# Reordering a cold-start stage and moving a logarithm off ScalarE: one change in two places of a spectral-mixing and memory-attention kernel

## The chip, the cores and the metric

One core of a Trainium2 chip. The metric is device time in microseconds (us), median of several executions. The classes are faster, same and slower at 2%.

## The reference, cut to what matters

Two pairs of layers over 2048 tokens of width 640, each layer reading a layer norm of the running x:

```python
x = A_x                                            # 2048 x 640, bf16
x = x + A(layernorm(x), A_w_r, A_w_i)              # rfft2, times a complex weight, irfft2
x = x + B(layernorm(x), mem0, Wq, Wk, Wv, Wo)      # 64 segments of 32 tokens + 8 memory tokens, 32 heads
x = x + A(layernorm(x), ...)
x = x + B(layernorm(x), ...)
# layernorm: (x - mean) / sqrt(var + 1e-5), without scale and bias
```

Most of the time is layer B's matmuls. The change concerns two things only: the start of the first layer A (the **cold stage**, from the start of the program until the first matmul of the spectrum, `ab`), and the layer norm between A and B (the two **token stages**, one for each pair of layers).

## The kernel before

The cold stage doesn't normalize x. It scales the DFT table of each 128-token tile by 1/sigma and takes the mean off with two small matmuls per tile. The 16 tiles fall into five rows, `groups`; a row's 1/sigma needs the statistics of all its tiles. Statistics come from VectorE (DVE) with `bn_stats` twice and `bn_aggr` once, or from two passes on ScalarE (ACT) for tiles 3, 7 and 11. The order of issue is written by hand:

```python
    def cold_raw(self, x_src, s3):
        ...
        groups = [(0, 4), (4, 8), (8, 12), (12, 14), (14, 16)]
        by_act = (3, 7, 11)
        ...
        def scales(q):
            a, b = groups[q]
            sl, v = slice(a, b), mv[:, a:b, 1]
            small = nc.gpsimd if q < 4 else nc.vector
            nc.scalar.activation(out=r0[:, sl], in_=v, func=ACTF.Ln, bias=g["eps"][:, 0:1])
            nc.scalar.activation(out=r0[:, sl], in_=r0[:, sl], func=ACTF.Exp, scale=-0.5)
            ...                       # one Newton step and the hi/lo parts of the mean, on `small`

        def stats(t):
            for hlf in range(2):
                nc.vector.bn_stats(out=st[:, t % 2, hlf, :], in_=x[:, t, hlf * 320:(hlf + 1) * 320])
            nc.vector.bn_aggr(out=mv[:, t, :], in_=st[:, t % 2, :, :])

        def scale_tables(q):
            for t in range(*groups[q]):
                nc.vector.tensor_scalar_mul(out=Ts[:, t, :], in0=T[:, t, :], scalar1=rs[:, t:t + 1])
        ...                           # matmuls(q): 60 (or 30) small matmuls; empties(q, ...): evictions of results from PSUM (PE's result memory), A = ACT, D = DVE
        with tc.manual_schedule(engines={...}):
            act_stats(3)
            for t in (0, 1, 2):
                stats(t)
            scales(0)
            ...
            act_stats(7)
            for t in (4, 5):
                stats(t)
            scale_tables(0)
            ps0 = matmuls(0)
            stats(6)
            scales(1)
            act_stats(11)
            for t in (8, 9):
                stats(t)
            scale_tables(1)
            empties(0, ps0, "AA")
            ps1 = matmuls(1)
            ...
            for t in (12, 13):
                stats(t)
            scales(3)
            ...
            empties(3, ps3, "AADAD")
            ps4 = matmuls(4)
            empties(4, ps4, "DADAD")
```

In a token stage tokens come in pairs. ACT evicts each token twice (`Gs` at L586, `x` at L603); DVE takes its statistics; `_ln_inverse` makes 1/sigma of the pair; DVE normalizes (`norm`, L130).

```python
def _ln_inverse(nc, pool, mv, nt, eps_t, small):
    ...
    nc.scalar.activation(out=r0, in_=mv[:, :nt, 1], func=ACTF.Ln, bias=eps_t[:, 0:1])     # L112
    nc.scalar.activation(out=r0, in_=r0, func=ACTF.Exp, scale=-0.5)                        # L113
    if small is nc.vector:
        ...                                                    # three instructions
    else:
        small.tensor_scalar_add(out=t, in0=mv[:, :nt, 1], scalar1=LN_EPS)                  # L120, then Newton
        small.tensor_tensor(out=t, in0=t, in1=r0, op=ALU.mult)
    small.tensor_tensor(out=t, in0=t, in1=r0, op=ALU.mult)
    small.tensor_scalar(out=t, in0=t, scalar1=-0.5, scalar2=1.5, op0=ALU.mult, op1=ALU.add)
    small.tensor_tensor(out=t, in0=t, in1=r0, op=ALU.mult)
...
            for i in range(16 + 1):                            # the token stage's order
                last = i >= 13
                if i >= 2 and last:
                    stats(i - 2)
                if i >= 5 and i % 2 == 1:
                    norm((i - 5) // 2)
                if i >= 2 and not last:
                    stats(i - 2)
                if i < 16:
                    spectrum_d(i)
                if 1 <= i <= 16:
                    tokens(i - 1)
                if i >= 4 and i % 2 == 0:
                    inverse((i - 4) // 2, nc.gpsimd)
```

## Time and profile before

| | before |
|---|---|
| median of 4 runs (lowest to highest) | 1559.09 us (1558.63 to 1559.90); the first three, which the prediction had, 1558.79 |
| span of the profiled execution | 1557.3 us |
| start to first `ab` matmul (S) | 26.56 us |
| first token stage (first psg to first psq matmul) | 42.54 us |
| second token stage | 42.55 us |

The last three rows are starts of matmuls, taken from the timeline of TensorE (PE). They are the lengths that the change can touch. The prediction below shows the page, the cold timeline and the chain of waits. Here is DVE's timeline in the cold stage (columns: start, length, engine, line, operation, output and input with their shapes, and in brackets the idle time before with its releaser):

```profile
7.79 0.89 DVE L313 BATCH_NORM_STATS2 A1xn_S<-A1x_S 128x6 f32<-128x320 bf16 x2 [0.74 <-DMA A1x_S<-in_A_x_dram]
8.71 0.21 DVE L314 BATCH_NORM_AGGREGATE A1xn_S<-A1xn_S 128x2 f32<-128x12 f32 x1
8.84 0.83 DVE L313 BATCH_NORM_STATS2 A1xn_S<-A1x_S 128x6 f32<-128x320 bf16 x2
```

Tile 4 reaches DVE 0.74 us late, from DRAM, while the tables of row 0 stand behind it in the queue.

### The profile page before, as it was taken

The page shows a single profiled execution, that of the slowest core. Times are in us where ns is not written, and L with a number is a line of the kernel's source. Part 1 is how long each engine was busy: PE and PEld are TensorE (multiplying, and loading weights), DVE is VectorE, ACT ScalarE, POOL GpSimd, SP SyncE. Part 2 cuts the span into 40 slices and gives each one's busy share as a digit, 9 for nine tenths or more (in the row PEclk, how much of TensorE's full clock was granted, in tenths as well). Part 3 has the DMA queues.
Part 4 walks back from the last instruction along what each step waited for, and adds up shares of the span by engine and source line. Part 5 has one row for each costly group of instructions (what it writes and reads, how often), then busy time and mean ns, then how long its engine had stood idle before and what let it go on. Part 6 is the DMA issues. An engine that isn't in the chain of part 4 may idle for free.

```text
span 1557.3 us, 36583 instructions
## 1 busy us (share of the span) xinstructions
PE 1531.2 (98%) x14482; PEld 1077.5 (69%) x14483; DVE 815.5 (52%) x2414; ACT 771.7 (50%) x2251; POOL 234.4 (15%) x327
## 2 busy tenths in 40 slices
PE   7999999999999999999999999999999999999998
PEld 5776666666666666777777776666666666667775
DVE  7873545665556555633367545655556545553111
ACT  5584555556555565511127655556555565562000
POOL 3520111112111121100034101112111121110000
PEclk9999999999999999999999999999999999999999
DMA  4681344444433433645114523443533434327241
GB/s 171 222 304 30 111 151 140 137 140 134 160 131 137 148 125 145 203 116 169 51 50 165 174 69 125 137 150 124 179 123 137 146 125 171 124 101 233 75 132 51
DMA packets 168694, 214.88 MB, mean 138 GB/s; under 512 B 8128, under 2 KB 134088, under 8 KB 168512
## 3 DMA queue, kind: packets, MB, share of 16 engines
q1 hardware_dynamic: 167936, 210.15, 41.0%
q8 instruction: 115, 1.88, 0.5%
q0 software_dynamic: 576, 2.30, 0.4%
q14 instruction: 67, 0.55, 0.1%
HBM read 167.32 MB, written 45.10 MB: 136 GB/s over the span
## 4 chain that ended last, share of the span: by engine, by line
PE 94%; DVE 2%; ACT 1%; DMA 1%; issue 1%; POOL 1%; SPq 0%; DVEq 0%; POOLq 0%; ACTq 0%
PE psv L1201 19%; PE psk L1135 18%; PE psx L1481 18%; PE psq L1135 18%; PE pso L1285 4%; PE pss L1211 4%; PE ab L427 2%; PE psg L585 1%; PE psl L1238 1%; PE psq L1159 1%; PE X L458 1%; PE psu L519 1%; PE psm L911 1%; DMA bB_S<-in_B_Wk_dram 1%; PE psg L1642 1%
## 5 line engine op out<-in xcount | busy, mean ns | idle before, releaser
L1135 PEld LDWEIGHTS <-bB_S 128*128 128x128 bf16 x3180 | 261.7, 97 | 181.6 <-DMA bB_S<-in_B_Wk_dram 1.1
L1194 DVE CAST bB_S<-psk 128x495 bf16<-128x495 f32 (+3 forms) x320 | 191.8, 599 | 281.2 <-PE psk L1135 276.7
L1481 PE MATMUL psx<-Wo_sb,bB_S 128*128 128x320 bf16 x2048 | 288.7, 299 | 0.1
L1214 ACT ACTIVATE bB_S<-pss 128x269 bf16<-128x269 f32 (+5 forms) x576 | 208.4, 386 | 138.2 <-PE pss L1211 137.9
L1481 PEld LDWEIGHTS <-bB_S 128*128 128x128 bf16 x2048 | 196.8, 98 | 73.9 <-DVE bB_S L1299 0.7
L1179 ACT ACTIVATE bB_S<-psq 128x96 bf16<-128x96 f32 x300 | 152.4, 508 | 172.2 <-PE psq L1135 172.2
L1254 POOL TENSOR_TENSOR bB_S<-bB_S,bB_S 128x535 f32<-128x535 f32 x90 | 111.7, 1255 | 795.2 <-DVE bB_S L1246 762.2
L1299 DVE TENSOR_TENSOR bB_S<-pso,bB_S 128x480 bf16<-128x480 f32 (+1 forms) x320 | 193.1, 603 | 55.6 <-PE pso L1285 44.9
L1215 DVE TENSOR_TENSOR bB_S<-bB_S,maskf 128x269 bf16<-128x269 bf16 (+5 forms) x576 | 159.4, 290 | 114.4 <-ACT bB_S L1214 114.4
L1203 ACT CAST bB_S<-psv 128x512 bf16<-128x512 f32 (+1 forms) x288 | 162.6, 564 | 80.9 <-PE psv L1201 80.9
L1201 PE MATMUL psv<-bB_S,B1hT_S 128*128 128x256 bf16 x1360 | 168.8, 272 | 0.0
L1201 PE MATMUL psv<-bB_S,B2hT_S 128*128 128x256 bf16 x1360 | 168.8, 272 | 0.0
L1135 PE MATMUL psk<-B2hT_S,bB_S 128*128 128x495 bf16 (+3 forms) x800 | 164.2, 343 | 0.0
L1135 PE MATMUL psk<-B1hT_S,bB_S 128*128 128x495 bf16 (+3 forms) x800 | 164.2, 343 | 0.0
L1135 PE MATMUL psq<-B1hT_S,bB_S 128*128 128x495 bf16 (+5 forms) x780 | 156.1, 336 | 0.6 <-DMA bB_S<-in_B_Wk_dram 0.5
L1135 PE MATMUL psq<-B2hT_S,bB_S 128*128 128x495 bf16 (+5 forms) x780 | 156.1, 336 | 0.5 <-DMA bB_S<-in_B_Wk_dram 0.5
L1201 PEld LDWEIGHTS <-B2hT_S 128*128 128x128 bf16 x1360 | 129.8, 98 | 24.3
L1201 PEld LDWEIGHTS <-B1hT_S 128*128 128x128 bf16 x1360 | 129.8, 98 | 24.3
L1211 PE MATMUL pss<-bB_S 128*128 128x132 bf16 (+8 forms) x1152 | 137.5, 219 | 0.0
L1211 PEld LDWEIGHTS <-bB_S 128*128 128x128 bf16 x1152 | 95.4, 97 | 55.1
L1285 PE MATMUL pso<-bB_S,bB_S 128*128 128x132 bf16 (+8 forms) x1152 | 118.6, 219 | 0.2
L1285 PEld LDWEIGHTS <-bB_S 128*128 128x128 bf16 x1152 | 89.7, 98 | 32.2 <-DVE oTmf L1300 1.8
(293 smaller groups left out, 1422.0 us busy)
## 6 DMA issues: line engine op xcount, KB each, us to landing
bB_S<-Rd SPq DMA_DIRECT2D x124, 535.0 KB
oTx_d<-bB_S SPq DMA_DIRECT2D x60, 512.0 KB
bB_S<-oTx_d SPq DMA_DIRECT2D x46, 512.0 KB
bB_S<-in_B_Wq_dram SPq DMA_DIRECT2D x32, 320.0 KB
bB_S<-in_B_Wk_dram SPq DMA_DIRECT2D x32, 320.0 KB
bB_S<-in_B_Wv_dram SPq DMA_DIRECT2D x32, 320.0 KB
Wo_sb<-in_B_Wo_dram SPq DMA_DIRECT2D x4, 1280.0 KB
B1wv_S<-in_B_Wv_dram SPq DMA_DIRECT2D x10, 512.0 KB
```

The lines of the kernel that those rows point to most:

```text
L1135: nc.tensor.matmul(ps, lhsT=w[:, ch, hh * 128:(hh + 1) * 128], rhs=src[:, ch, lo:hi], start=(ch == 0), stop=(ch == 4))
L1179: nc.scalar.mul(out=qv[:, :, 0:SEG], in_=x_view(ps, o, n)[:, :, 1:SW], mul=scale)
L1194: nc.vector.tensor_copy(out=KTs[h % 2][:, lo:hi], in_=ps[:, 0:hi - lo])
L1201: nc.tensor.matmul(ps[:, i * 256:(i + 1) * 256], lhsT=hT[:, ch, st.hcol((t + i) * 128):st.hcol((t + i) * 128) + 128], rhs=w["Wv"][:, ch, : ...
L1203: nc.scalar.copy(out=V[:, t:t + n, :].rearrange("p a b -> p (a b)"), in_=ps[:, 0:n * 256])
L1211: nc.tensor.matmul(ps[:, off - o0:off - o0 + hi - lo], lhsT=KT[:, t * 128:(t + 1) * 128], rhs=QT[:, lo:hi], start=True, stop=True)
L1214: nc.scalar.activation(out=E[:, 0:n], in_=ps[:, 0:n], func=ACTF.Exp)
L1215: nc.vector.tensor_tensor(out=P[:, o0:o0 + n], in0=E[:, 0:n], in1=bs.mask[:, o0:o0 + n], op=ALU.mult)
L1254: nc.gpsimd.tensor_tensor(out=acc, in0=acc, in1=part, op=ALU.add)
L1285: nc.tensor.matmul(pso[:, lo - q0:hi - q0], lhsT=V[:, t, (h % 2) * 128:(h % 2 + 1) * 128], rhs=P[:, off:off + hi - lo], start=(i == 0), st ...
L1299: nc.vector.tensor_tensor(out=oT.rearrange("p (r s j) -> p r s j", r=16, j=2)[:, :, s0:s0 + ns, :], in0=byclass(po), in1=rx, op=ALU.mult)
L1481: self.tc.nc.tensor.matmul(ps[:, 0:320], lhsT=lhs(h, k // 2), rhs=self.g["Wo_sb"][:, h, c0:c0 + 320], start=(h == 0), stop=(h == H - 1))
```

## The change

Its intent: in the cold stage, let PE start earlier and at full clock, and keep DVE and ACT from waiting for one another; in the token stages, take the logarithm and the exponential out of ACT's queue by computing (var + eps)^-0.5 with `pow` on GpSimd. The core of the diff:

```diff
+def _inverse(nc, g, t, r0, v, small):
     if small is nc.vector:
+        nc.scalar.activation(out=r0, in_=v, func=ACTF.Ln, bias=g["eps"][:, 0:1])
+        nc.scalar.activation(out=r0, in_=r0, func=ACTF.Exp, scale=-0.5)
         ...
+        return
+    small.tensor_scalar_add(out=t, in0=v, scalar1=LN_EPS)
+    small.tensor_tensor(out=r0, in0=t, in1=g["half"][:, 0:t.shape[1]], op=ALU.pow)    # half holds -0.5
+    small.tensor_tensor(out=t, in0=t, in1=r0, op=ALU.mult)                            # Newton step as before
     ...
-            if a in (4, 8):                       # loads of the tables
-                nc.sync.dma_start(out=T[:, 2 * a - 8:2 * a, :], ...)
+            if a in (2, 4, 8):
+                c, d = (a // 4 * 4, b) if a < 8 else (8, 16)
+                nc.sync.dma_start(out=T[:, c:d, :], ...)
-        by_act = (3, 7, 11)
+        by_act = (3, 7, 11, 13)
+        idle = pp.tile([128, 4, 128], FP32, name="idle", tag="pa")
+        for i in range(WARM):                     # WARM = 96
+            nc.tensor.matmul(idle[:, i % 4, :], lhsT=g["ones"][:], rhs=g["ones"][:], start=True, stop=True)
+        def logs(q):                              # Ln and Exp of a row, now on their own
+            flush()
+            ...
         def scales(q):
-            small = nc.gpsimd if q < 4 else nc.vector
-            ...                                   # Ln, Exp; Newton on small
+            ...                                   # Newton on DVE, means on GpSimd
         def stats(t):
-            for hlf in range(2):
-                nc.vector.bn_stats(out=st[:, t % 2, hlf, :], ...)
-            nc.vector.bn_aggr(out=mv[:, t, :], in_=st[:, t % 2, :, :])
+            nc.vector.bn_stats(out=st[:, t % 2, 0, :], ...)
+            flush()                               # the bn_aggr of the tile before
+            nc.vector.bn_stats(out=st[:, t % 2, 1, :], ...)
+            pending.append(t)
         def scale_tables(q):                      # tables 2 and 3 of row 0 go to ACT
-            act_stats(7)
-            for t in (4, 5):
-                stats(t)
             scale_tables(0)
             ps0 = matmuls(0)
-            stats(6)
+            act_stats(7)
+            for t in (4, 5, 6):
+                stats(t)
+            logs(1)
+            stats(8)
             scales(1)
+            scale_tables(1)
+            ps1 = matmuls(1)
+            empties(0, ps0, "AA")
+            act_stats(11)
             ...                                   # likewise for rows 2 to 4: logs(q), one more tile, scales(q)
+            act_stats(13)
+            logs(3)
```

More of the change, by code (lines that the diff above doesn't have):

```diff
@@ L20 @@
 S, D = 2048, 640
+WARM = 96
 NF = 321
@@ L105, in _ln_stats, with _ln_inverse @@
     nc.vector.bn_aggr(out=mv[:, t, :], in_=st[:, t % 2, :, :])
-def _ln_inverse(nc, pool, mv, nt, eps_t, small):
+def _ln_inverse(nc, pool, mv, nt, g, small):
     rs = pool.tile([128, 4], FP32, name="lnrs", tag="lnrs", bufs=3)
     nb = pool.tile([128, 4], FP32, name="lnnb", tag="lnnb", bufs=3)
-    t, r0 = rs[:, :nt], nb[:, :nt]
-    nc.scalar.activation(out=r0, in_=mv[:, :nt, 1], func=ACTF.Ln, bias=eps_t[:, 0:1])
-    nc.scalar.activation(out=r0, in_=r0, func=ACTF.Exp, scale=-0.5)
+    _inverse(nc, g, rs[:, :nt], nb[:, :nt], mv[:, :nt, 1], small)
+    return rs, nb
+def _inverse(nc, g, t, r0, v, small):
     if small is nc.vector:
-        small.scalar_tensor_tensor(out=t, in0=mv[:, :nt, 1], scalar=LN_EPS, in1=r0, op0=ALU.add, op1=ALU.mult)
+        nc.scalar.activation(out=r0, in_=v, func=ACTF.Ln, bias=g["eps"][:, 0:1])
+        nc.scalar.activation(out=r0, in_=r0, func=ACTF.Exp, scale=-0.5)
+        small.scalar_tensor_tensor(out=t, in0=v, scalar=LN_EPS, in1=r0, op0=ALU.add, op1=ALU.mult)
         small.scalar_tensor_tensor(out=t, in0=t, scalar=-0.5, in1=r0, op0=ALU.mult, op1=ALU.mult)
         small.scalar_tensor_tensor(out=t, in0=t, scalar=1.5, in1=r0, op0=ALU.add, op1=ALU.mult)
-        return rs, nb
-    else:
-        small.tensor_scalar_add(out=t, in0=mv[:, :nt, 1], scalar1=LN_EPS)
-        small.tensor_tensor(out=t, in0=t, in1=r0, op=ALU.mult)
+        return
+    small.tensor_scalar_add(out=t, in0=v, scalar1=LN_EPS)
+    small.tensor_tensor(out=r0, in0=t, in1=g["half"][:, 0:t.shape[1]], op=ALU.pow)
+    small.tensor_tensor(out=t, in0=t, in1=r0, op=ALU.mult)
     small.tensor_tensor(out=t, in0=t, in1=r0, op=ALU.mult)
@@ L124, in _ln_inverse @@
     small.tensor_tensor(out=t, in0=t, in1=r0, op=ALU.mult)
-    return rs, nb
 def _ln_scale(nc, mv, rs, xin, xout, nt):
@@ L130, in _ln_scale, with _ln_apply @@
         nc.vector.tensor_scalar(out=xout[:, t, :], in0=xin[:, t, :], scalar1=mv[:, t, 0:1], scalar2=rs[:, t:t + 1], op0=ALU.subtract, op1=ALU.mult)
-def _ln_apply(nc, pool, mv, xin, xout, nt, eps_t, on_dve=False):
-    rs, nb = _ln_inverse(nc, pool, mv, nt, eps_t, nc.vector)
+def _ln_apply(nc, pool, mv, xin, xout, nt, g, on_dve=False):
+    rs, nb = _ln_inverse(nc, pool, mv, nt, g, nc.vector)
     if on_dve:
@@ L278, in cold_raw @@
             nc.sync.dma_start(out=x[:, a:b, :], in_=r16(x_src)[:, a:b, :])
-            if a in (4, 8):
-                nc.sync.dma_start(out=T[:, 2 * a - 8:2 * a, :], in_=g["cd"]["cT"][:, 2 * a - 8:2 * a, :])
+            if a in (2, 4, 8):
+                c, d = (a // 4 * 4, b) if a < 8 else (8, 16)
+                nc.sync.dma_start(out=T[:, c:d, :], in_=g["cd"]["cT"][:, c:d, :])
         groups = [(0, 4), (4, 8), (8, 12), (12, 14), (14, 16)]
-        by_act = (3, 7, 11)
+        by_act = (3, 7, 11, 13)
         pp = tc.alloc_tile_pool(name=f"{self.lname}_ps1", bufs=8, space=PSUM)
+        idle = pp.tile([128, 4, 128], FP32, name="idle", tag="pa")
+        for i in range(WARM):
+            nc.tensor.matmul(idle[:, i % 4, :], lhsT=g["ones"][:], rhs=g["ones"][:], start=True, stop=True)
         def act_stats(t):
@@ L287, in act_stats @@
             nc.scalar.activation(out=scr[:, 1, :], in_=x[:, t, :], func=ACTF.Square, scale=D ** -0.5, bias=nm[:, t:t + 1], accum_out=mv[:, t, 1:2])
+        def logs(q):
+            flush()
+            sl = slice(*groups[q])
+            nc.scalar.activation(out=r0[:, sl], in_=mv[:, sl, 1], func=ACTF.Ln, bias=g["eps"][:, 0:1])
+            nc.scalar.activation(out=r0[:, sl], in_=r0[:, sl], func=ACTF.Exp, scale=-0.5)
         def scales(q):
@@ L291, in scales @@
             sl, v = slice(a, b), mv[:, a:b, 1]
-            small = nc.gpsimd if q < 4 else nc.vector
-            nc.scalar.activation(out=r0[:, sl], in_=v, func=ACTF.Ln, bias=g["eps"][:, 0:1])
-            nc.scalar.activation(out=r0[:, sl], in_=r0[:, sl], func=ACTF.Exp, scale=-0.5)
+            small = nc.gpsimd
             n = b - 1 if b - 1 in by_act else b
+            t, r = rs[:, sl], r0[:, sl]
+            nc.vector.scalar_tensor_tensor(out=t, in0=v, scalar=LN_EPS, in1=r, op0=ALU.add, op1=ALU.mult)
+            nc.vector.scalar_tensor_tensor(out=t, in0=t, scalar=-0.5, in1=r, op0=ALU.mult, op1=ALU.mult)
+            nc.vector.scalar_tensor_tensor(out=t, in0=t, scalar=1.5, in1=r, op0=ALU.add, op1=ALU.mult)
             small.tensor_scalar_mul(out=mn[:, a:n], in0=mv[:, a:n, 0], scalar1=-1.0)
@@ L298, in scales, with flush @@
                 small.tensor_scalar_mul(out=mn[:, n:b], in0=nm[:, n:b], scalar1=D ** 0.5)
-            t, r = rs[:, sl], r0[:, sl]
-            if small is nc.gpsimd:
-                small.tensor_scalar_add(out=t, in0=v, scalar1=LN_EPS)
-                small.tensor_tensor(out=t, in0=t, in1=r, op=ALU.mult)
-            else:
-                small.scalar_tensor_tensor(out=t, in0=v, scalar=LN_EPS, in1=r, op0=ALU.add, op1=ALU.mult)
-            small.tensor_tensor(out=t, in0=t, in1=r, op=ALU.mult)
-            small.tensor_scalar(out=t, in0=t, scalar1=-0.5, scalar2=1.5, op0=ALU.mult, op1=ALU.add)
-            small.tensor_tensor(out=t, in0=t, in1=r, op=ALU.mult)
             small.tensor_copy(out=mh[:, sl, 0], in_=mn[:, sl])
             small.tensor_tensor(out=mh[:, sl, 1], in0=mn[:, sl], in1=mh[:, sl, 0], op=ALU.subtract)
+        pending = []
+        def flush():
+            if pending:
+                t = pending.pop()
+                nc.vector.bn_aggr(out=mv[:, t, :], in_=st[:, t % 2, :, :])
         def stats(t):
-            for hlf in range(2):
-                nc.vector.bn_stats(out=st[:, t % 2, hlf, :], in_=x[:, t, hlf * 320:(hlf + 1) * 320])
-            nc.vector.bn_aggr(out=mv[:, t, :], in_=st[:, t % 2, :, :])
+            nc.vector.bn_stats(out=st[:, t % 2, 0, :], in_=x[:, t, 0:320])
+            flush()
+            nc.vector.bn_stats(out=st[:, t % 2, 1, :], in_=x[:, t, 320:640])
+            pending.append(t)
         def scale_tables(q):
             for t in range(*groups[q]):
-                nc.vector.tensor_scalar_mul(out=Ts[:, t, :], in0=T[:, t, :], scalar1=rs[:, t:t + 1])
+                if q or t < 2:
+                    nc.vector.tensor_scalar_mul(out=Ts[:, t, :], in0=T[:, t, :], scalar1=rs[:, t:t + 1])
+                else:
+                    nc.scalar.mul(out=Ts[:, t, :], in_=T[:, t, :], mul=rs[:, t:t + 1])
         def matmuls(q):
@@ L349, in cold_raw @@
                 stats(t)
+            logs(0)
             scales(0)
@@ L352, in cold_raw @@
             self.load_mirror(0)
-            act_stats(7)
-            for t in (4, 5):
-                stats(t)
             scale_tables(0)
             ps0 = matmuls(0)
-            stats(6)
+            act_stats(7)
[3 more added lines that the diff above has]
+            stats(8)
             scales(1)
             self.load_mirror(1)
+            scale_tables(1)
+            ps1 = matmuls(1)
+            empties(0, ps0, "AA")
             act_stats(11)
-            for t in (8, 9):
+            for t in (9, 10):
                 stats(t)
-            scale_tables(1)
-            empties(0, ps0, "AA")
-            ps1 = matmuls(1)
-            stats(10)
+            empties(0, ps0, "  AAA")
+            logs(2)
+            stats(12)
             scales(2)
-            empties(0, ps0, "  AAA")
-            for t in (12, 13):
-                stats(t)
-            scales(3)
-            empties(1, ps1, "AA")
             scale_tables(2)
             ps2 = matmuls(2)
+            act_stats(13)
+            logs(3)
+            empties(1, ps1, "AA")
             stats(14)
-            stats(15)
+            scales(3)
             scale_tables(3)
-            scales(4)
             empties(1, ps1, "  AAA")
             ps3 = matmuls(3)
+            stats(15)
+            logs(4)
+            scales(4)
             scale_tables(4)
@@ L620, in inverse @@
         def inverse(q, small):
-            rs[q], _ = _ln_inverse(nc, wk, mv[q], 2, g["eps"], small)
+            rs[q], _ = _ln_inverse(nc, wk, mv[q], 2, g, small)
         def norm(q):
@@ L974, in run @@
                 xno = wk.tile([128, 1, D], BF16, name="xno", tag="xno")
-                _ln_apply(nc, wk, mv, xo, xno, 1, self.g["eps"], on_dve=True)
+                _ln_apply(nc, wk, mv, xo, xno, 1, self.g, on_dve=True)
                 nc.sync.dma_start(out=self.xnd[:, t, :], in_=xno[:, 0, :])
@@ L1501, in run @@
                 _ln_stats(nc, st, mv, x[:, t, :], 0)
-                _ln_apply(nc, self.g["ln"], mv, x[:, t:t + 1, :], xns[t % 3].unsqueeze(1), 1, self.g["eps"], on_dve=True)
+                _ln_apply(nc, self.g["ln"], mv, x[:, t:t + 1, :], xns[t % 3].unsqueeze(1), 1, self.g, on_dve=True)
             if t == 2:
@@ L1681, in make_globals @@
     nc.vector.memset(g["eps"][:], LN_EPS)
+    g["half"] = sp.tile([128, 4], FP32, name="half")
+    nc.vector.memset(g["half"][:], -0.5)
     g["floor"] = sp.tile([128, 1], FP32, name="floor")
```

## The prediction

> **What bounds the kernel now.** I read the page first: the busy shares and the chain that ended last.
>
> ```profile
> span 1557.3 us, 36583 instructions
> PE 1531.2 (98%) x14482; PEld 1077.5 (69%) x14483; DVE 815.5 (52%) x2414; ACT 771.7 (50%) x2251; POOL 234.4 (15%) x327
> ...
> PE 94%; DVE 2%; ACT 1%; DMA 1%; issue 1%; POOL 1%; SPq 0%; DVEq 0%; POOLq 0%; ACTq 0%
> ```
>
> TensorE (PE) is on 94% of the path. The change doesn't touch its real work, so only the rest, some 90 us, is open to it, and of that only the stretches that the edited code owns: the cold stage (from the start to the first matmul of the spectrum) and the two token stages. Next, the timeline of the cold stage, cut to what sets its pace:
>
> ```profile
> 9.83 0.75 DVE L318 TENSOR_SCALAR A1xn_S<-A1xn_S 128x128 bf16<-128x128 bf16 x4
> ...
> 10.15 1.60 PE L327 MATMUL ps<-A1xn_S,A1x_S 128*128 128x128 bf16 x12 [10.15 <-DVE A1xn_S L318]
> ...
> 11.71 0.30 ACT L293 ACTIVATE A1xn_S<-A1xn_S,eps 128x4 f32<-128x4 f32 x1 [2.22 <-DVE A1xn_S L314]
> ...
> 15.13 0.83 PE L327 MATMUL ps<-A1xn_S,A1x_S 128*128 128x128 bf16 x12
> ...
> 18.48 0.83 PE L327 MATMUL ps<-A1xn_S,A1x_S 128*128 128x128 bf16 x12
> ...
> 20.42 0.29 ACT L293 ACTIVATE A1xn_S<-A1xn_S,eps 128x2 f32<-128x2 f32 x1 [1.22 <-DVE A1xn_S L314]
> ...
> 20.86 3.83 ACT L265 CAST A1YT_S<-ps 128x512 bf16<-128x512 f32 x9
> ...
> 26.56 2.92 PE L427 MATMUL ab<-A1tab_S,A1YT_S 128*128 128x321 bf16 x20 [0.52 <-DVE A1YT_S L265]
> ```
>
> Columns are start, length, engine, line, operation, and in brackets the idle time just before and its releaser. PE starts at 10.15 on the first scaled tables, runs rows 0, 1 and 2 without a gap (10.15, 15.13, 18.48), and from 22.0 is held by PSUM: ScalarE (ACT) has nine evictions to do from 20.86. The stage ends at 26.56. ACT stood idle 2.22 us and 1.22 us waiting for statistics.
>
> Last, the chain of waits in the first token stage, at the two places where it leaves PE:
>
> ```profile
> 94.36 0.31 ACT lnnb L112
> ...
> 94.69 0.21 ACT lnnb L113
> ...
> 95.04 0.20 POOL lnrs L121
> ...
> 96.10 0.81 DVE A1tok_S L130 x2
> ...
> 103.21 0.59 ACT A1tok_S L586
> ...
> 105.94 0.20 POOL lnrs L121
> ...
> 108.62 0.81 DVE A1tok_S L130 x2
> ```
>
> The logarithm and exponential on ACT (L112, L113) release GpSimd (POOL), then VectorE (DVE) L130, then PE. Elsewhere this stage is bound by PE: 1.65 us a token, back to back. The second token stage repeats it at 858.18 and 866.50.
>
> **What the Trainium skill says.** "TensorE: Matmul & The Clock Gate", Part 1, says that an idle array runs at half clock and gets full clock after about 3.4 us of activity. The trace agrees: the first 12 row matmuls take 1.60 us, the same 12 of row 1 take 0.83, and the change comes at about 13.5 us, 3.4 after the start. The same page, "Engine queue depths", says ACT and DVE are strict first-in first-out; the trace agrees: at 20.42 ACT had sat 1.22 us behind one logarithm with evictions queued after it. [...]No page gives a time for pow on POOL, and no instruction of the trace shows one.
>
> **Part 1, dummy matmuls and the first tables.** 96 dummies can start at about 1.2 us (the ones tile is written at 0.92 to 1.09). Estimate from the trace: 31 cold at 0.107 until about 4.6, then 65 at 0.057, so they end near 8.3; if the clock comes later, by 10. For row 0: statistics of tile 2 end at about 7.0 as now, logarithm and exponential at 7.6 (0.30 + 0.03 + 0.20 + waits), three DVE steps at 0.20 in place of five POOL steps (8.2 instead of 9.3), tables at once rather than after two more tiles. First real matmul at about 8.6, against 10.15. At full clock row 0's 60 matmuls take 3.4 instead of 5.0, so row 0 ends at 12.2 instead of 15.1. That is 2.9 us gained at this point.
>
> **Part 2, where it goes.** Row 1 needs the statistics of tile 6 (DVE, after tables 0: three tiles at 0.97, so 8.7 + 3.0 = 11.7, unchanged from 11.71). Then Ln and Exp 0.54, three DVE steps 0.6, first table 0.3: row 1 starts at 13.4 and ends at 17. From 11.75 ACT has no idle time any more. Its queue with its durations from the trace (a 512-wide eviction 0.52, a 256-wide 0.37, a pair of statistics passes 1.68, Ln and Exp 0.54): Ln/Exp of row 1 to 12.3; two evictions 13.3; tile 11 15.0; three evictions 16.55; Ln/Exp of row 2 17.1; tile 13, newly on ACT, 18.8; Ln/Exp of row 3 19.35; five evictions of row 1 21.95; Ln/Exp of row 4 22.5; three evictions of row 2 24.05. Today those last three end at 20.86 + 6 x 0.52 = 24.0. So row 2 starts near 18.0 (18.48 now), stalls for row 1's banks, and the banks that row 4 needs come free no earlier. DVE's two evictions of row 2 also move from 22.3 to about 23.5, behind the later tables of row 4. Laid out the same way, the old order comes out 0.35 late against the trace, and the new one 0.1 later than the old. The one-later aggregation saves about 0.05 us a tile (0.99 to 0.94), 0.6 in all, on DVE, which isn't last here. Cold stage: **+0.1, taken as -0.2 with some credit to an order that was presumably tried**; between -1.2 and +0.8.
>
> **Part 3, token norms.** In seven of eight pairs per stage Ln and Exp (0.50 us, 0.55 with issue) leave ACT and one pow of length p is added on POOL. The six POOL steps need only the variance. First place: the variance is ready at 93.76 and L120 ends at 94.07, so the chain ends at 94.14 + p + 0.07 + 1.03 = 95.24 + p instead of 96.07; PE's stall there (pstr takes 1.07 instead of 0.61) falls by up to 0.5. Second place: L586 at 103.11 comes earlier by what L112 and L113 took, 0.44, of a PE wait of 0.53: gain 0.4. Tail: L120 ends at 105.29, the chain at 106.4 + p with the mean step between (0.28) at 106.7 + p, against 107.29; the last two L130 and the weight loads behind them come about 0.3 earlier at p = 0.25, hardly at p = 0.6. For p = 0.25 to 0.5 (an estimate, near the other small POOL steps with some more arithmetic): 0.5 + 0.4 + 0.2 = 1.1 a stage, of which I take 0.85 as some will meet the weight DMA after the tail (PE waits 0.45 for it today). Two stages: **-1.7**.
>
> Sum: 1558.8 - 0.2 - 1.7 = **1556.9 us**.
>
> **Rivals.** First: pow is a slow routine on POOL. With p = 1.0 the first place still gains, the tail loses 0.4, and a stage gains 0.3: about 1558. With p = 2 or more each chain is over 3.4 us, as long as a pair of tokens (3.3), DVE waits at each pair: 1 to 3 us lost a stage, 1560 to 1564. For it: a general power is no single arithmetic step, and nothing here times it. Against: only two elements a partition, and POOL is idle about 2 us a pair. Second: the cold order gains what it means to. If PE paced the stage, 2.9 us at row 0 would come through less about 1.4 of new gaps, so -1.5: total 1555.4. For it: PE is on the chain now. Against: ACT's queue above. Third: the changed order costs, because tile 13's passes on ACT hold row 1's banks and PE idles in rows 2 to 4: +0.8, about 1558. Fourth: the token gain is hidden by the weight DMA after it: the loads go out after the last store, so they move with it, but the 16 engines are near full from 112 to 116 us. It would cut half of the tail's part, 0.1 to 0.2 a stage.
>
> **Range and chances.** The parts are 0.1% of the time, so within 2% is all but sure. Best mix (cold -1.2, tokens -2.4): 1555.2. Worst likely mix (cold +0.6, tokens 0): 1559.4. So 1555.3 to 1559.2 for 8 in 10. Over 2% (31 us) would need a stage to break down: 0.01 for faster, 0.01 for slower, 0.98 same.
>
> **What would show it.** In the changed profile: dummies from about 1.2 to 8.3 us; first table matmul at 8.6 +- 0.5 at pitch 0.057; row 1 at 13.4 after an idle of over 1 us; ACT without a wait from 12 to 24; the spectrum's first matmul within 0.8 us of 26.56. In the token stages, pow at 0.25 to 0.5 us, no L112/L113 but the last pair's, PE's wait of 0.53 for L586 nearly gone, and the first matmul after each stage's weights about 0.85 us closer to that stage's start. Wrong would be: a pow over 1 us; a spectrum that starts before 25.5 us; or row 1 not waiting for tile 6.

## More of the kernel before

Next, GpSimd's (POOL's) timeline at the first pair of the first token stage:

```profile
80.37 0.23 POOL L120 TENSOR_SCALAR lnrs<-lnmv 128x2 f32<-128x2 f32 x1 [9.23 <-DVE lnmv L105]
83.00 0.19 POOL L121 TENSOR_TENSOR lnrs<-lnrs,lnnb 128x2 f32<-128x2 f32 x1 [2.40 <-ACT lnnb L113]
```

The variance is there at 80.3, and POOL then waits 2.40 us for ACT, whose logarithm stands in its queue behind evictions until 82.32.

## The result, and the profile after

| | before | after | difference |
|---|---|---|---|
| median | 1559.09 us | 1555.86 us (1555.63 to 1555.95, 4 runs) | -3.2 us |
| ratio, 95% interval | | 0.9979 (0.9961 to 0.9996) | class: same |
| start to first `ab` matmul (S) | 26.56 | 25.65 | -0.91 |
| first token stage | 42.54 | 41.44 | -1.10 |
| second token stage | 42.55 | 41.40 | -1.15 |
| all the rest of the span | 1445.65 | 1445.61 | 0.0 |

A ratio, here and below, is the mean time of one kernel's fast runs over that of the other's of the same rounds, so not quite the ratio of the medians. The prediction was 1556.9 with a range of 1555.3 to 1559.2. The time fell in the range and in the class it gave 0.98. The 0.0 for the rest is chance: from trace to trace it varies by 1.2 us. But the cold stage gave 0.9 where it took 0.2, and the token stages 2.25 where it took 1.7.

The page of the kernel after:

```profile
PE 1536.6 (99%) x14578; PEld 1083.0 (70%) x14579; DVE 814.9 (52%) x2418; ACT 769.9 (50%) x2229; POOL 242.9 (16%) x325
...
PE 92%; DVE 4%; POOL 1%; ACT 1%; issue 1%; DMA 0%; DVEq 0%; ACTq 0%; POOLq 0%
```

PE's busy time grew by 5.4 us although the program is 3.2 us shorter: the 96 dummies are 7.0 us of it. DVE's share of the last chain rose from 2% to 4%, a first hint at who sets the pace where PE doesn't. PE's timeline in the cold stage after:

```profile
1.17 7.01 PE L291 MATMUL idle<-ones 128*128 128x128 bf16 x96 [1.17 <-DVE ones L1716]
8.31 1.10 PE L345 MATMUL ps<-A1xn_S,A1x_S 128*128 128x128 bf16 x12
...
12.91 1.35 PE L345 MATMUL ps<-A1xn_S,A1x_S 128*128 128x128 bf16 x12 [0.82 <-DVE A1xn_S L334]
...
17.35 1.25 PE L345 MATMUL ps<-A1xn_S,A1x_S 128*128 128x128 bf16 x12 [0.41 <-DMA A1tab_S<-in_A_w_i_dram]
```

Row 0 starts 1.84 us earlier than before, at full clock (8 matmuls of the next line take 0.61 us, as late in the stage before). Row 1 starts 2.22 earlier, row 2 (18.48 before) only 1.13, the spectrum 0.91: the gain at the front shrinks, as it does when PE isn't what sets the pace. (The DMA in brackets before row 2 is doubtful: its tile isn't an operand of that matmul, DVE began row 2's tables at 16.95, and the trace of e7 names DVE at the same place.) ACT's timeline after shows what does:

```profile
11.27 0.30 ACT L300 ACTIVATE A1xn_S<-A1xn_S,eps 128x4 f32<-128x4 f32 x1 [0.90 <-DVE A1xn_S L323]
...
18.53 2.52 ACT L269 CAST A1YT_S<-ps 128x512 bf16<-128x512 f32 x5
...
24.39 0.37 ACT L269 CAST A1YT_S<-ps 128x256 bf16<-128x256 f32 x1 [0.61 <-PE ps L350]
```

From row 1's logarithm at 11.27 until 23.8 ACT has no wait; the next is the 0.61 us before 24.39. Everything ACT does in those 12.5 us follows from when that logarithm starts, and it starts when DVE has the statistics of tile 6 (`L323` is the aggregation).

In the token stages, POOL's timeline at the first pair, and the waits of PE over the whole first stage (72 to 118 us; columns: who waited for whom, us in total, times, longest):

```profile
79.46 0.25 POOL L124 TENSOR_SCALAR lnrs<-lnmv 128x2 f32<-128x2 f32 x1 [9.22 <-DVE lnmv L106]
79.79 0.73 POOL L125 TENSOR_TENSOR lnnb<-lnrs,half 128x2 f32<-128x2 f32 x1
```

```profile
PE psu L1574 <- DVE A1tok_S L134: 0.9, 2, 0.7
PE psq L1157 <- DVE bB_S L1602: 0.5, 1, 0.5
```

The `pow` takes 0.73 us, and the 2.40 us of waiting for ACT are gone. Of PE's waits, the 0.53 for L586 has gone, and so has the stretched `pstr` group (1.07 us at 96.34 before, 0.61 at 95.27 now). Those are 0.53 + 0.46 = 0.99 of the 1.10 us. The two waits for the norms of the tail (`psu`, 0.9 in total) are as long as before.

### The profile page after: what moved, and what is told of

Same layout as the page of the kernel before. It is cut to its first block, busy times and chain, and to the rows that moved or that the text cites. A ratio compares the mean times of both kernels' runs of the same rounds, so it can differ in the third digit from the quotient of the medians.

```text
span 1554.1 us, 36747 instructions
## 1 busy us (share of the span) xinstructions
PE 1536.6 (99%) x14578; PEld 1083.0 (70%) x14579; DVE 814.9 (52%) x2418; ACT 769.9 (50%) x2229; POOL 242.9 (16%) x325
## 4 chain that ended last, share of the span: by engine, by line
PE 92%; DVE 4%; POOL 1%; ACT 1%; issue 1%; DMA 0%; DVEq 0%; ACTq 0%; POOLq 0%
PE psv L1223 19%; PE psk L1157 19%; PE psx L1503 18%; PE psq L1157 18%; PE pso L1307 4%; PE pss L1233 4%; PE ab L449 2%; PE psl L1260 1%; PE psq L1181 1%; DVE lnst L105 1%; PE X L480 1%; PE psu L541 1%; PE psm L933 1%; PE psg L1664 1%; PE psvb L1596 1%
## 5 line engine op out<-in xcount | busy, mean ns | idle before, releaser
L1223 PEld LDWEIGHTS <-B1hT_S 128*128 128x128 bf16 x1360 | 129.8, 98 | 24.3
L1223 PEld LDWEIGHTS <-B2hT_S 128*128 128x128 bf16 x1360 | 129.8, 98 | 24.3
```

The lines of the kernel that those rows point to most:

```text
L1223: nc.tensor.matmul(ps[:, i * 256:(i + 1) * 256], lhsT=hT[:, ch, st.hcol((t + i) * 128):st.hcol((t + i) * 128) + 128], rhs=w["Wv"][:, ch, : ...
```

## The experiments

Whole times resolve little here: a ratio of four runs to the runs before has an interval of about plus or minus 0.17%, or 2.6 us, and the parts are under 2.5 us; the class of all twelve is "same". e1 to e4, e5 to e8 and e9 to e12 ran on three different chips, each set beside the kernel before. So each run is read by its segments. The token stages repeat to 0.1 us between kernels with the same code. The cold stage doesn't: x arrives from DRAM at slightly different times. The table therefore gives, besides S, when DVE starts its first `bn_stats`, how long DVE waited for tile 4, and when row 1's logarithm started on ACT.

| kernel | first bn_stats | wait for tile 4 | first table matmul | row 1 logarithm | S | S minus logarithm | token stages | median us | ratio to before |
|---|---|---|---|---|---|---|---|---|---|
| before | 3.93 | 0.74 | 10.15 | 11.71 | 26.56 | 14.85 | 42.54, 42.55 | 1559.09 | |
| after | 3.83 | none | 8.31 | 11.27 | 25.65 | 14.38 | 41.44, 41.40 | 1555.86 | 0.9979 |
| e1 pow only | 3.91 | none | 9.60 | 11.21 | 26.66 | 15.45 | 41.36, 41.36 | 1556.51 | 0.9984 |
| e2 cold only | 3.95 | none | 8.76 | 11.38 | 25.75 | 14.37 | 42.55, 42.55 | 1557.61 | 0.9991 |
| e3 aggr back | 3.98 | none | 8.72 | 11.94 | 26.44 | 14.50 | 41.37, 41.34 | 1556.23 | 0.9982 |
| e4 no dummies | 4.00 | none | 8.47 | 11.43 | 25.80 | 14.37 | 41.39, 41.38 | 1555.85 | 0.9986 |
| e5 tile 13 on DVE | 4.04 | 0.39 | 8.50 | 11.94 | 28.63 | 16.69 | 41.36, 41.37 | 1556.86 | 0.9983 |
| e6 pow twice | 3.99 | 0.19 | 8.46 | 11.71 | 26.07 | 14.36 | 46.16, 46.47 | 1563.97 | 1.0029 |
| e7 pow, no Newton | 3.89 | none | 8.37 | 11.31 | 25.68 | 14.37 | 40.69, 40.69 | 1554.43 | 0.9968 |
| e8 pow everywhere | 3.98 | none | 8.72 | none on ACT | 26.32 | | 40.70, 40.69 | 1554.54 | 0.9969 |
| e9 before, aggr later | 3.93 | none | 9.35 | 11.03 | 26.00 | 14.97 | 42.52, 42.53 | 1559.33 | 0.9999 |
| e10 before, dummies | 3.97 | 0.78 | 10.18 | 11.75 | 26.43 | 14.68 | 42.54, 42.53 | 1558.30 | 0.9991 |
| e11 before, both | 3.93 | 0.87 | 9.61 | 11.24 | 26.05 | 14.81 | 42.53, 42.53 | 1558.05 | 0.9990 |
| e12 e7 + eviction moved | 3.88 | none | 9.07 | 11.31 | 25.74 | 14.43 | 40.68, 40.69 | 1553.78 | 0.9963 |

The token stages of e6 contain a half-clock spell each (see there). All runs agreed with the reference. The rest of the span (everything but S and the token stages, with 47.3 us of spectrum) varies by 1.2 us from trace to trace without pattern.

Read the column "S minus logarithm" first. Six kernels with the changed order (after, e2, e4, e6, e7, e12) give 14.36 to 14.43, while the logarithm itself moves from 11.27 to 11.71. In the changed order, S is the start of row 1's logarithm plus a constant. When PE starts doesn't enter: in e12 the dummies ran until 9.2, so the first table matmul came 0.76 us later than in the kernel after, and the difference is 14.43. In the old order (before, e1, e9 to e11) the difference wanders from 14.68 to 15.45, so there the logarithm is not the whole story.

### e1 and e2: one half of the change each

e1 puts the `pow` into the kernel before and leaves its cold stage alone:

```diff
-    nc.scalar.activation(out=r0, in_=mv[:, :nt, 1], func=ACTF.Ln, bias=eps_t[:, 0:1])
-    nc.scalar.activation(out=r0, in_=r0, func=ACTF.Exp, scale=-0.5)
     if small is nc.vector:
+        nc.scalar.activation(...Ln...); nc.scalar.activation(...Exp...)
     ...
     small.tensor_scalar_add(out=t, in0=mv[:, :nt, 1], scalar1=LN_EPS)
+    small.tensor_tensor(out=r0, in0=t, in1=HALF[0][:, 0:nt], op=ALU.pow)
```

> The kernel before with only the token norms' pow. My theory (the changes are two separate gains that add): the spectrum still starts at 26.56 us, each token stage up to the first psq matmul goes from 42.4 to 41.3 us, in all -2.2 us against before. Rival (the token gain needs the earlier start, by the phase of the weight DMA): less than -1.5 us.

e2 is the kernel after with the logarithm and exponential put back in the token norms:

```diff
     small.tensor_scalar_add(out=t, in0=v, scalar1=LN_EPS)
-    small.tensor_tensor(out=r0, in0=t, in1=g["half"][:, 0:t.shape[1]], op=ALU.pow)
+    (Ln and Exp of v on ACT, ahead of it)
```

> The changed kernel with the token norms put back on the logarithm and exponential. My theory: the spectrum starts at 25.65 us, the token stages take 42.4 us each as before, in all -0.9 us against before. Rival (part of the cold gain came from elsewhere): the start of the spectrum lands at another time than 25.65, or the token stages stay near 41.3 us.

The halves are separate and add up. e1 has the token stages of the kernel after (41.36) and an old cold stage (26.66); e2 has the old token stages (42.55) and the new cold stage (25.75). The token stages give 1.1 to 1.2 us each, the cold stage 0.8 to 0.9.

e1 holds a warning too. Its tile 4 came without a wait, PE started 0.55 us earlier than in the kernel before, and row 1's logarithm was 0.50 earlier; S was nevertheless 0.10 later. PE's timeline of e1 shows why:

```profile
13.60 2.49 PE L334 MATMUL ps<-A1xn_S 128*128 128x128 bf16 x24
```

In the kernel before the same 24 matmuls take 1.50 us, from 13.79. By the pitch of the matmuls (0.104 us at half clock, 0.056 at full) e1's half clock lasted from 9.60 to about 15.7, that of the kernel before from 10.15 to about 13.5. PE then ran without any wait until the end of e1's cold stage. So in the old order PE and the ACT-DVE chain are about level, and the length of the cold spell, which differs between executions of identical code, can decide.

### e3: the aggregation put back

```diff
         def stats(t):
             nc.vector.bn_stats(out=st[:, t % 2, 0, :], ...)
-            flush()
             nc.vector.bn_stats(out=st[:, t % 2, 1, :], ...)
             pending.append(t)
+            flush()
```

> The changed kernel with each bn_aggr put right behind its second bn_stats. Theory A (VectorE's pace over tiles 4 to 6 sets when ScalarE's full queue begins, and I mis-sized that pace): tile pitch on VectorE goes from 0.86 back to about 0.99 us, the row 1 logarithm from 11.27 to about 11.7, and the start of the spectrum moves 0.4 to 0.6 later. Rival B (ScalarE's queue is full and hides it, as my prediction held): start of the spectrum within 0.15 us of 25.65.

S rose by 0.79 us. Here is a tile on DVE in the kernel after, then the same in e3:

```profile
9.14 0.47 DVE L326 BATCH_NORM_STATS2 A1xn_S<-A1x_S 128x6 f32<-128x320 bf16 x1
9.53 0.19 DVE L323 BATCH_NORM_AGGREGATE A1xn_S<-A1xn_S 128x2 f32<-128x12 f32 x1
9.64 0.44 DVE L328 BATCH_NORM_STATS2 A1xn_S<-A1x_S 128x6 f32<-128x320 bf16 x1
9.99 0.48 DVE L326 BATCH_NORM_STATS2 A1xn_S<-A1x_S 128x6 f32<-128x320 bf16 x1
```

```profile
9.15 0.48 DVE L327 BATCH_NORM_STATS2 A1xn_S<-A1x_S 128x6 f32<-128x320 bf16 x1
9.66 0.21 DVE L323 BATCH_NORM_AGGREGATE A1xn_S<-A1xn_S 128x2 f32<-128x12 f32 x1
9.78 0.44 DVE L326 BATCH_NORM_STATS2 A1xn_S<-A1x_S 128x6 f32<-128x320 bf16 x1
```

Read the starts, not the lengths. An instruction that doesn't need the one before starts 0.35 to 0.39 us after it, while that one (0.44 to 0.48 long) is still in its last 0.1 us. The aggregation that needs it starts 0.51 after it: it waits for the end and 0.03 more. A tile costs 0.85 us with an independent instruction between (9.14 to 9.99) and 0.99 without (9.78 to 10.77 in e3): 0.14 us, not 0.05.

Then follow it to S. Row 1's logarithm started at 11.94 in place of 11.27: 0.67 later, of which 0.15 is x's later arrival (3.98 against 3.83), so 0.52 by the order. The rest of ACT's queue shifted with it, and from the logarithm to S another 0.12 was lost (14.50 against 14.38). In total S is 0.64 us worse, net of the arrival; more than either theory expected, and about three quarters of what the cold half of the change gained (0.87 us net of arrival, see e9 to e11).

### e4: no dummy matmuls

```diff
-WARM = 96
+WARM = 0
-        idle = pp.tile([128, 4, 128], FP32, name="idle", tag="pa")
```

> The changed kernel without the 96 dummy matmuls. Theory A (TensorE isn't what paces the cold stage: row 1 waits for its tables at 12.9): row 0 runs at half clock to about 13.3 instead of 12.1, row 1 starts 0.4 later, and the start of the spectrum stays within 0.3 us of 25.65. Rival B (the dummies are where the 0.91 us comes from): the spectrum starts 0.9 us or more later.

S was 25.80, which looks like a loss of 0.15. But DVE's first statistics came 0.17 later, and S minus logarithm is 14.37, the constant. In this run row 0 ran at half clock until about 13.2 and lasted from 8.47 to 14.1, in place of 8.31 to 12.1, and row 1 started at 14.12 in place of 12.91 (1.2 later, where 0.4 was expected); by row 2 (17.51 against 17.35) only the later arrival was left. So in the changed order the dummies won 2 us at the end of row 0 and none at S. What they may be worth in an execution with a longer cold spell, like e1's, isn't shown. Three of e4's four executions took 1555.74 to 1555.86, like the kernel after; the fourth, which has no profile, took 1559.21.

### e5: tile 13's statistics back on DVE

```diff
-        by_act = (3, 7, 11, 13)
+        by_act = (3, 7, 11)
-            act_stats(13)
+            stats(13)
```

> The changed kernel with tile 13's statistics back on VectorE, at the same place in the order. Theory A (VectorE's statistics are the pace, so a tile on ScalarE relieves it): the row 3 logarithm, at 18.09 us, moves later or stays, and the start of the spectrum moves 0.3 to 0.9 us later than 25.65. Rival B (my prediction's third rival: tile 13 on ScalarE holds the evictions of row 1): the spectrum starts 0.3 us or more earlier.

S rose by 2.98 us. Of that, 0.67 isn't the edit's: row 1's logarithm was at 11.94, because tile 4 arrived at 9.00 after a wait of 0.39. S minus logarithm is 16.69, so 2.3 us belong to the edit and what it set off. Row 3's logarithm waited 2.69 us for DVE and started at 19.68 (18.09 after), so the evictions of row 1 started at 20.11 in place of 18.53, and PE waited for one. PE's timeline of e5:

```profile
20.73 0.45 PE L345 MATMUL ps<-A1xn_S,A1x_S 128*128 128x128 bf16 x4 [1.04 <-ACT A1YT_S L269]
20.98 1.06 PE L350 MATMUL ps<-A1xn_S 128*128 128x128 bf16 x8
...
22.26 2.50 PE L350 MATMUL ps<-A1xn_S 128*128 128x128 bf16 x24
```

The same groups of 8 and 24 take 0.61 and 1.50 in the kernel after. The windows view of e5 (columns: window, length, busy time of PE, PEld, DVE, ACT and POOL with numbers of instructions, granted clock, DMA share, GB/s) confirms it in its clock column:

```profile
18.00:20.00 2.00, 1.65 (x20) 1.29 (x21) 1.97 (x9) 0.29 (x1) 0.24 (x1) 1.00 0.94 319
...
22.00:23.00 1.00, 1.00 (x12) 1.00 (x10) 0.37 (x2) 0.97 (x5) 0.41 (x2) 0.50 0.00 0
```

PE's clock was halved from about 20.9 to 24.3 us, directly after that wait. The work from 20.73 to 24.59, 3.86 us, takes 2.23 in the kernel after (19.15 to 21.38): 1.6 of the 2.3 us. So the direct cost of leaving tile 13 on DVE is about 0.7 us, and a chance that PE's wait costs a half-clock spell. It doesn't seem to come each time: the profiled execution is the slowest of the four (1558.16 us at a mean granted clock of 0.998), and two others took 1556.23 and 1556.37 at 0.999. Longer waits of PE, such as the 1.28 us before row 1 in e3, had none.

### e9, e10, e11: the aggregation, the dummies and both, alone in the kernel before

e9 has the new `stats` with `flush()` at the start of `scales`; e10 the idle tile and 96 dummies ahead of the stage; e11 both. The edits are the lines of the change above.

> The kernel before with bn_aggr one operation later and nothing else. Theory A (in the old order TensorE, cold and without a gap from 10.15 to 22.0 us, paces the stage, so VectorE's saving is hidden): the spectrum starts within 0.25 us of 26.56. Theory B (the saving counts in any order): 0.6 to 0.9 us earlier.

> The kernel before with the 96 dummy matmuls and nothing else. Theory A (TensorE paced the old order, so a warm array passes the pace on to the next engine): the first scaled matmul stays at about 10.1, row 0 ends 1.5 us earlier, the spectrum starts 0.2 to 0.8 us earlier than 26.56. Theory B (as in the changed order, where taking them out cost 0.15): within 0.2 us.

> The kernel before with the dummies and bn_aggr one operation later, without the new order. If the two together are the whole cold gain: the spectrum starts within 0.2 us of 25.65. If the new order (tables before tiles 4 to 6, tile 13 on ScalarE) is needed: 26.0 or later.

S was 26.00, 26.43 and 26.05 against 26.56 (and 26.66 in e1). The later aggregation helps in the old order too, by up to 0.56, but its size there can't be settled from these traces: e9's tile 4 came without a wait and PE started 0.80 earlier than in the kernel before, partly for that reason. The cleanest pair is e10 and e11, which both waited for tile 4 and both started warm: 0.38 us, of which up to 0.21 may be tile 4's earlier arrival (7.65 against 7.86). The dummies alone gave 0.13, and nothing that is seen on top of the aggregation (26.05 against 26.00). By the ratios the whole times say nothing at this size: e9's is 0.9999 plus or minus 0.0017. Yet all eight executions of e10 and e11 (1557.78 to 1558.39) are shorter than all seven of the kernel before in the same rounds (from 1558.61) and all four of e9 (from 1558.85). About 1 us seems to go with the dummies in the old order, more than the 0.13 at S; in the profiled executions most of that difference lies in the rest of the span, and where it comes from isn't shown.

The rest of the new order can be bounded: e3 has everything new but the aggregation. Counted from the first `bn_stats`, its S is 22.46, against 22.63 and 22.75 in the two old-order runs (before and e1) and 21.82 after. So of 0.87 us (the mean of the two, 22.69, less 21.82), 0.64 came with the aggregation and about 0.2 with all else, and 0.2 is twice the difference between two runs of the same old stage.

### e6: the pow doubled

```diff
     small.tensor_tensor(out=r0, in0=t, in1=g["half"]..., op=ALU.pow)
+    small.tensor_tensor(out=r0, in0=t, in1=g["half"]..., op=ALU.pow)
```

> The changed kernel with the token norms' pow done twice in a row (same output), so 1.5 us instead of 0.73. Theory A (only the tail's last GpSimd chain is on the path; in the loop the chain has slack): each token stage takes 0.6 to 0.9 us more than 41.4. Theory B (my prediction's first rival: a longer chain makes VectorE wait at each pair): 1.5 us more or worse a stage. Theory C (all is hidden): within 0.2 us.

The stages grew by 4.7 and 5.1 us. Not all of that is the chain: the windows view of e6 shows PE's clock halved at the end of both stages, after waits of 1.91 and 1.90 us for the norms (columns as in e5):

```profile
111.00:114.00 3.00, 2.85 (x33) 2.78 (x33) 1.53 (x4) 1.97 (x5) 0.46 (x9) 0.50 0.91 293
879.00:882.00 3.00, 3.00 (x40) 3.00 (x39) 2.01 (x6) 2.94 (x6) 0.46 (x9) 0.50 0.93 294
```

Each spell lasted 3.4 us and cost 1.1 and 1.4 us: from the first `pstrb` matmul to psq pass 7.78 and 8.21 us, against 6.78 in the kernel after, and in the first stage the group ahead of it took 0.1 more. That leaves 3.6 us a stage for the chain. Seven pairs have a second `pow` of 0.70 us, 4.9 in all: about three quarters of it came through, as theory B said. The profiled execution is also the slowest of the four (1565.59; the others 1563.51 to 1564.04). The chain of waits of e6 (start, length, engine, tile, line) has left PE for nearly the whole loop:

```profile
89.95 0.72 POOL lnnb L125
90.73 0.70 POOL lnnb L126
...
92.56 0.80 DVE A1tok_S L135 x2
...
97.41 0.80 DVE A1tok_S L135 x2
```

From norm to norm 4.85 us pass: norm 0.80, `bn_stats` 0.81 and `bn_aggr` 0.22 of the next pair's second token, then on POOL the addition, two `pow`s and four Newton steps. This is a recurrence on DVE: the norm of one pair stands in DVE's queue before the statistics of a later token. Without the second `pow` it is about 4.1 us, and in the kernel after the norms of the first three pairs start at 81.67, 85.78 and 90.03, at just such a distance. So the kernel after runs with this loop at the edge: it is hidden, but nothing is left over.

### e7: the pow without the Newton step

```diff
-    small.tensor_tensor(out=r0, in0=t, in1=g["half"]..., op=ALU.pow)
-    (four instructions of the Newton step)
+    small.tensor_tensor(out=t, in0=t, in1=g["half"]..., op=ALU.pow)
```

> The changed kernel without the four GpSimd steps that refine pow in the token norms (a Newton step): result must stay right to the reference, if pow is exact enough. The chain is 1.1 us shorter. If the tail's chain is on the path: each token stage 0.3 to 0.6 us shorter than 41.4 (then ScalarE's statistics of the last tile bound the tail). If the loop and ScalarE set it: within 0.15 us.

Both stages shrank by 0.7 to 0.75 us more, to 40.69, above the 0.3 to 0.6 expected, and the result still agrees with the reference: for this check the `pow` doesn't need the refinement that the logarithm and exponential had. The chain is four instructions, 1.1 us, shorter. The loop takes no less than in the kernel after (102.57 - 73.00 = 29.57 us to the tail, 102.54 - 72.96 = 29.58 there), so the gain is in the tail: PE's waits for the norms (`psu`) fall from 0.9 to 0.5 us, the 20 matmuls around the first of them take 0.75 us in place of 0.46 and 0.68, and the last norm starts 0.7 earlier (105.89 against 106.61).

### e8: the pow in the cold stage as well

```diff
         def logs(q):
             flush()
-            (Ln and Exp on ACT)
         def scales(q):
-            (three instructions on VectorE)
+            small.tensor_scalar_add(out=r, in0=v, scalar1=LN_EPS)
+            small.tensor_tensor(out=t, in0=r, in1=g["half"][:, 0:b - a], op=ALU.pow)
```

> As the run without the refining steps, and in the cold stage too GpSimd's add and pow in place of ScalarE's logarithm and exponential and VectorE's three steps. If statistics on VectorE and the full ScalarE queue are the pace: ScalarE loses 5 x 0.54 us and VectorE 5 x 0.6 us, so the spectrum starts 0.7 to 1.5 us before 25.65. Rival (GpSimd's chain, 0.3 + 0.8 us and the means after it, takes the place of the old chain): within 0.3 us of 25.65.

The token stages are e7's, and the cold stage is 0.5 us worse (22.34 from the first `bn_stats`, against 21.79 in e7), later than both expectations allowed. POOL's timeline of e8:

```profile
7.34 1.04 POOL L304 TENSOR_TENSOR A1xn_S<-A1xn_S,half 128x4 f32<-128x4 f32 x1
...
19.06 0.73 POOL L304 TENSOR_TENSOR A1xn_S<-A1xn_S,half 128x2 f32<-128x2 f32 x1
```

A `pow` of four elements a partition takes 1.04 us and one of two 0.73, so that row 0's 1/sigma takes POOL 1.4 us (7.00 to 8.38), where in the kernel after ACT and DVE need 1.2 (6.78 to 7.98). In exchange ACT isn't full any more (it waits 0.41, 0.87 and 1.60 us from 19.4 on), and at the end of the stage it is PE that waits, for DVE's evictions. The chain through POOL took the place of the one through ACT.

### e12: e7 with one eviction moved

```diff
-            empties(4, ps4, "DADAD")
+            empties(4, ps4, "AADAD")
```

> A candidate for the best: pow without the refining steps in the token norms (40.7 us a stage) and, at the end of the cold stage, the first eviction of the last row on ScalarE, which sits idle 0.61 us there, in place of VectorE. Spectrum at 25.4 to 25.6 instead of 25.68 if VectorE's last seven evictions are the bound, 25.65 or later if the matmuls before them are; in all 1554.3 us, give or take 0.4.

S is 25.74, e7's within the noise: the last matmuls, not the evictions, are what the end waits for. Its whole time of 1553.78 us (1553.66 to 1554.04; ratio 0.9963, 0.9946 to 0.9980) is the lowest, 0.1 below the range expected. The 0.65 us below e7 lie in the rest of the span, in which kernels with the same code differ as much. So what beats both kernels with a cause shown is the omission of the Newton step: about 1.45 us below the kernel after.

## Why the prediction was right, and where its sizes were wrong

The total fell in the range, and the main mechanisms held: the token gain is real, the early start of PE is lost again, and ACT's queue is full. But two terms of the sum were too small, and that the token term came as near as it did (1.7 for 2.25) is partly luck: with the `pow` as long as it turned out, the prediction's own formula gives some 0.5 a stage, 1.0 in all.

**The failed step: "The one-later aggregation saves about 0.05 us a tile (0.99 to 0.94), 0.6 in all, on DVE, which isn't last here."** It saves 0.14 us a tile, and DVE is last: its statistics release row 1's logarithm. Undone, it costs 0.64 us of S net of x's arrival (e3); the whole term was taken as 0.2 and measured 0.91. The prediction said correctly that ACT has no idle time after row 1's logarithm. But it took that logarithm to be "unchanged from 11.71". A full queue hides a gain that comes after its beginning; one that comes before its beginning goes through whole. Six of DVE's tiles lie before it, and four of them have another tile's `bn_stats` to put between: 4 times 0.13 to 0.14 is the 0.52 by which e3's logarithm was later.

**What else was said of the cold stage.** The dummies end at 8.2 (8.3 predicted), the first table matmul is at 8.31 (8.6), row 0 ends at 12.1 (12.2), and ACT is without a wait from 12 to 24: right. Row 1 starts at 12.91 after 0.82 idle (13.4, over 1 us), row 2 at 17.35 (18.0), the spectrum at 25.65 (26.36 taken, "within 0.8 us of 26.56", missed by 0.1): all earlier than predicted, by 0.49, 0.65 and 0.71. 0.44 of it is that logarithm; the rest is the layout of ACT's queue, which came out too long, as the prediction noted of the old order (0.35). That the dummies' gain isn't seen at S is shown by e4. The "wrong would be" mark of a spectrum before 25.5 was not reached.

**The token stages.** The `pow` took 0.73 us, beyond the 0.25 to 0.5 of the estimate, and yet a stage gained 1.1, the worked-out value for the shorter `pow`. Put p = 0.73 into the prediction's own formula and the first place gains only 0.1 (95.24 + 0.73 = 95.97 against 96.07). What the formula had wrong is "the variance is ready at 93.76", held fixed. Through the recurrence on DVE an earlier norm makes the next variance earlier. Counted from the stage's first psg matmul, the first norm starts 1.47 us earlier (84.06 - 73.88 = 10.18 before, 81.67 - 72.96 = 8.71 after), for the logarithm no longer stands behind evictions on ACT; the second 0.98, and all later ones 0.98 to 1.09. And the variances of the second, third and fourth pair reach POOL 1.47, 0.98 and 0.98 earlier, each by just as much as the norm before it. So both stalls of PE at pstr and L586 go entirely, 0.99 us, at p = 0.73. That they would go at any p below the loop's bound is argued and not shown. The tail behaved as said: no gain at this p. And the discount from 1.1 to 0.85 "as some will meet the weight DMA" was wrong: PE's wait of 0.45 before the next layer's psq is there in all versions, and the whole gain of the tail passed through in e7.

**The rivals.** The first (a slow `pow`) put 1 to 3 us of loss at p = 2 or more. The shape is right, and it sets in earlier: with p = 1.4 in two parts, e6 loses 3.6 a stage against the kernel after, or 2.5 against the kernel before, both net of the half-clock spells (4.7 to 5.1 and 3.6 to 3.9 with them). The second (the cold order gains what it means to, 1.5) is wrong in its reason, PE's early start, as e4 shows; the measured 0.9 lies between it and the prediction because DVE gave what PE didn't. The third (tile 13 on ACT costs) is contradicted: putting it back on DVE costs about 0.7 us, and 2.3 with the half-clock spell it met (e5). The fourth (hidden by the weight DMA) didn't occur: the stages are measured to behind that wait, and it is 0.45 us in both.

**What stays open.** How much the later aggregation gives in the old order (0.2 to 0.6); why the half-clock spell lasted 3.1 to 6.1 us in different executions, and why the waits in e5 and e6 were followed by one and those in e3 and e10 weren't; what the dummies do to the whole time in the old order; and what moves the rest of the span by up to 1.2 us. One follow-up wasn't tried: the token norms' `_ln_stats` still aggregates right behind its `bn_stats`, in the loop that e6 showed to be at the edge.

## What to carry to other kernels

When an engine's queue is full, look for the instruction that its full stretch starts with, and ask who releases that one: gains ahead of it come through whole, gains behind it vanish. Measure an instruction's cost from start to start, once with an independent and once with a dependent successor; and where one engine's work for step n stands ahead of its work for step n+1, treat the loop as a recurrence and don't hold its inputs fixed when you estimate. For effects under 0.2% read segments of the trace, and tie them to an event inside the stage, since data arrival and the clock move the raw times as much as the change does.

## What the Trainium skill lacked or had wrong

- No page gives a time for `pow` on GpSimd; "GPSIMD Engine Reference", section 3.1, counts elementwise work at about 2.6 cycles an element plus dispatch. Here `pow` takes 0.73 us at 2 and 1.04 us at 4 elements a partition, where a multiplication of the same shape takes 0.20: some 0.15 us for each further element.
- "VectorE: DVE Perf Modes", "The DRAIN you can't avoid", says that an operation starts once the pipe of the one before has emptied, and that a semaphore between them cost nothing extra in its measurement of copies. Here an independent successor starts 0.35 to 0.40 us after a `bn_stats` of 0.44 to 0.48, before its recorded end, and a dependent `bn_aggr` 0.51 after it: dependence costs 0.12 to 0.14 us, 0.64 us of this stage. The section does note that some successors start earlier, without a number.
- "TensorE: Matmul & The Clock Gate", Part 1, gives about 3.4 us of activity to full clock, run-variable in the number of matmuls, and puts the change around 4 us, 0.5 either way. Here the half-clock spell lasted about 3.1 us (e9), 3.3 (before), 4.8 (e4) and 6.1 (e1) of uninterrupted matmuls: the time varies by more than that. The page warns that clock events in traces can't be fully trusted on trn2; here the record of the granted clock reads 1.00 all through these first spells, where a matmul starts each 0.104 us instead of each 0.056, and only the later spells of e5 and e6 show in it.
- The same page lists half clock after an idle window of about 3.4 us; its section "A second HAM failure mode: psum-queue depth-cycling" has frequent short idles between groups make the clock swing too. Here half clock (0.50 in the record, for 3.4 us each time) followed shorter waits: 1.04 us for an eviction (e5), and 1.91 and 1.90 us for a norm (e6, where it began 1.0 and 1.8 us after the wait). Waits of 1.28 us (e3) and 1.56 us (before the first table matmul of e10) were not followed by it. So the length of one wait doesn't tell, and no run here shows what does.
